# First blocks of a windowed attention: keys and queries split in three column parts, POOL's order written out, masks in one operation each, and products of zeros in TensorE's waits

## The chip, the core and the metric

The kernel runs on one core of a Trainium2 chip. The metric is the device time of one execution in microseconds (us). Besides, one execution was taken by the hardware profiler; its rows name engines as PE (TensorE matmul), PEld (TensorE weight load), DVE (VectorE), ACT (ScalarE), POOL (GpSimd) and SP (SyncE, which issues most loads).

## The reference

Attention over 4 batches of 8 heads, 768 positions of 64 numbers, where a query sees the 128 newest positions and 4 sink positions at the start; behind it a mixture of experts, in which a token may keep its predecessor's expert.

```python
def _attn_ref(q, k, v, n_sink, window):
    scores = scale * np.matmul(q, k.transpose(0, 1, 3, 2))
    is_sink = pos[None, :] < int(n_sink)
    rel = pos[:, None] - pos[None, :]
    in_window = (rel >= 0) & (rel < int(window))
    scores = np.where(is_sink | in_window, scores, -1000000000.0)
    a = np.exp(scores - np.max(scores, axis=-1, keepdims=True))
    a = a / (np.sum(a, axis=-1, keepdims=True) + 1e-09)
    return np.matmul(a, v)

def _moe_ref(x, w_gate, w_local, w1, w2):   # for each token
    e = fresh_e if s == 0 or local_gate[b, s] < 0.5 else prev_e
    h = np.maximum(x[b, s] @ w1[e], 0.0)
    out[b, s] = p[e] * (h @ w2[e])
```

## The kernel before

The attention runs in 8 groups (batch, half of the heads), each of 6 blocks of 128 queries, 48 blocks in all; the experts follow. A group has two pairs of heads, and a block two units, one for each pair. For a unit, `score` makes three products for each head: high part of the queries with high and low part of the keys, and low part of the queries with the high part of the keys. High parts are casts of the raw numbers (L132), low parts are raw minus high (L137). `out` adds the mask and takes the extreme (DVE, L616) and makes exponentials with their sums (ACT, L619). One block later `turn` transposes them (L634) and ACT copies them out of PSUM (L641); two blocks later `apply` multiplies with the values (L665, L670), three blocks later `back` and `finish` turn and scale the result (L560, L576). The order of PE, DVE and ACT in the loop over blocks is the program's; POOL's was left to the compiler's scheduler.

Raw keys and queries of a pair lie in one of four buffers and are loaded in one transfer; for group 0 in two, columns 0 to 255 (`lead`) and the rest. Which engine casts and subtracts for group 0 is in `SENG`: keys cast by DVE, subtracted by POOL, queries cast by ACT, subtracted by DVE. From group 1 on POOL does all four steps of a pair (`ENGS`); group 1's are called at blocks 3 to 5 (`HEADS`), and block 6 is the first that reads them. The keys of the sink positions meet their values in a product of their own, for which POOL prepares the value rows (`sinks`, L548 and L549) after a load of 96 KB. `setup` and `xb_meta` are small copies on POOL for the routing. Before the first block PE runs 12 products of zeros (L183), and DVE makes three masks (L206 to L214), mask2 for blocks 2 to 5, mask1 for block 1, mask0 for block 0.

Of the kernel before, what the change touches and what calls it, by code (L numbers as in the profile page):

```python
# [27 lines left out]
SK = 8  # L28
# [3 lines left out]
ROW = 516  # L32
SKIP = 1 << 20
# [39 lines left out]
def kernel(ctx, tc, qkd, vn, vs, w1, w2, nw, c_misc, c_ident, c_idw, c_small,  # L73
# [60 lines left out]
    lows, behind = {}, []  # L134

    def low(e, out, raw, hi):
        lows[e] = getattr(nc, e).tensor_tensor(out=out, in0=raw, in1=hi.bitcast(F32), op=ALU.subtract)  # L137

    def qk_split(gi, eng, ahead=True, qc=slice(0, S), kc=slice(0, KPAD)):
        def part(p, x, cs, eng):  # L140
            hi, lo = qk_t[gi % 2][p][2 * x:2 * x + 2]
            r = raw[(gi * NPR + p) % NR][:, x]
            i = copy(eng[0], hi[:, cs], r[:, cs])
# [3 lines left out]
            low(eng[1], lo[:, cs], r[:, cs], hi[:, cs])  # L147

        def keys(p):
            part(p, 1, kc, eng[p][0:2])  # L150

        def queries(p):
            part(p, 0, qc, eng[p][2:4])
            if ahead:
                qk_load(gi * NPR + p + NR)

        steps = []
        for p in range(NPR):
            steps += [lambda p=p: keys(p), lambda p=p: queries(p)]
        heads = [[(qh, kh), (qh, kl), (ql, kh)] for qh, ql, kh, kl in qk_t[gi % 2]]  # L160
        return steps, heads

    lead = 2 * P
# [3 lines left out]
    qk_load(0, slice(0, lead))  # L167
    qk_load(1, slice(0, lead))
# [4 lines left out]
    nc.sync.dma_start(v_t[0][:, 2:NBLK], vn[0, 0, :, 2:NBLK])  # L173

    zrow = const.tile([P, ROW], F32, name="zrow")
    nc.gpsimd.memset(zrow, 0.0)
    nc.gpsimd.memset(zrow.bitcast(I32)[:, 513:514], SKIP)

    with tc.tile_pool(name="ps_w", bufs=1, space=PS) as ps_w:
        wt = ps_w.tile([P, 512], F32, name="wt")  # L180
        zb = zrow.bitcast(BF16)
# [22 lines left out]
    mask = at.tile([P, N2 + 3 * P], F32, name="mask")  # L204
    mask2, mask1, mask0 = mask[:, 0:N2], mask[:, N2:N2 + 2 * P], mask[:, N2 + 2 * P:]
    nc.vector.tensor_scalar(mask2, rel, win, None, op0=ALU.is_lt)  # L206
    nc.vector.scalar_tensor_tensor(out=mask2, in0=rel, scalar=0.0, in1=mask2, op0=ALU.is_ge, op1=ALU.mult)
    nc.vector.tensor_scalar(mask2[:, P:P + SK], key, nsk, None, op0=ALU.is_lt)
    nc.vector.tensor_copy(mask1[:, 0:P], mask2[:, 0:P])
    nc.vector.tensor_copy(mask1[:, P:2 * P], mask2[:, P + SK:N2])  # L210
    nc.vector.tensor_copy(mask0, mask2[:, P + SK:N2])
    for m in (mask1, mask0):
        nc.vector.tensor_tensor(out=m[:, 0:SK], in0=m[:, 0:SK], in1=mask2[:, P:P + SK], op=ALU.max)
    nc.vector.tensor_scalar(mask, mask, BIG, -BIG, op0=ALU.mult, op1=ALU.add)  # L214

    lead0, heads0 = qk_split(0, SENG, False, slice(0, lead), slice(0, lead))
    rest0 = qk_split(0, SENG, False, slice(lead, S), slice(lead, KPAD))[0]
    with tc.issue_after(flag_op.ins) if FLAGF else ExitStack():
        for f in lead0[0:2]:
            f()  # L220

    narrow = nc.values_load(flag_i[0:1, 0:1], min_val=0, max_val=1,
                            skip_runtime_bounds_check_because="a product of comparisons")
# [234 lines left out]
    def xb_meta(b):  # L458
        xb = xb_t[b % 2]
        nc.gpsimd.tensor_copy(xb.bitcast(I32)[:, :, DM + 1], ids[:, b * NBLK:(b + 1) * NBLK])  # L460
        nc.gpsimd.memset(xb[:, :, DM + 2:ROW], 0.0)
# [50 lines left out]
    def attention(fast):  # L512
        sfx = "f" if fast else "g"
        with ExitStack() as st:
# [225 lines left out]

            if fast:
                ng = len(groups)
                preps = [{"heads": []} for _ in groups]
                preps[0]["heads"] = heads0
                gst = [group_steps(b, g, preps[gi]) for gi, (b, g) in enumerate(groups)]

                def head(gi, h):
                    if h == 0:
                        preps[gi]["steps"], preps[gi]["heads"] = qk_split(gi, ENGS)
                    preps[gi]["steps"][h]()  # L750

                def slot(u, gi, k):
                    nx = gi + 1
                    if gi == 0:
                        for x in LOADS.get(k, ()):
                            qk_load(x) if x > 1 else gst[nx]["load"][x]()
                        if k == RK:
                            gst[0]["sinks"]()
# [12 lines left out]
                    if gi:  # L771
                        last.clear()
# [27 lines left out]
                for b in range(B - 1):  # L800
# [6 lines left out]
                for f in lead0[2:]:  # L807
                    f()
                order = ExitStack()
                order.enter_context(tc.manual_schedule(engines={ET.PE, ET.DVE, ET.Activation}))  # L810

                for n in range(nb):
                    now, a, z, y = (blocks[x] if 0 <= x < nb else [] for x in (n, n - 1, n - 2, n - 3))
                    nm = f"{sfx}{n}"
                    deep = bool(a) and a[0]["i"] >= 2
                    for u in now:
                        if u["k"] == 0 and u["g"] == 0 and n:
                            xb_meta(u["b"])
                        if u["gi"] == 0 and u["k"] == 6:
                            xb_meta(0)  # L820
# [20 lines left out]
                    if a:  # L841
                        turned(a[0])
                    lo = sink_out(a[0]["blk"], tps, mm, nm) if deep else None
                    if now:
                        out(now[1])
                    for _, read, _ in todo:
# [7 lines left out]
                        lo()  # L854
                    if a:
                        invert(a[0]["blk"])
                    if n < 2:
                        for f in rest0[2 * n:2 * n + 2]:
                            f()
                    for u in now:  # L860
                        slot(u, u["gi"], u["k"])
                    if z:
# [541 lines left out]
def _layout(q, k, v, w_gate, w_local, w1, w2, n_sink, window):  # L1404
# [19 lines left out]
    p = np.arange(P)[:, None]  # L1424
    c = np.arange(P)[None, :]
    s = np.zeros((P, SK))
    rel = np.concatenate([P + p - c, s - 1, p - c], axis=1).astype(f)
# [34 lines left out]
```

## Time and profile before

| | us |
|---|---|
| median of 3 runs | 561.14 |
| lowest, highest | 560.61, 565.27 |
| the profiled execution's own time | 567.39 |
| its span, first to last instruction | 565.6 |

The profiled execution is one run, and not the fastest; durations of single instructions are read from it. Its mean granted TensorE clock is 0.963 of full speed (2.4 GHz); 0.50 means 1.2 GHz. In a timeline row the first number is the start in us from the span's start, the second the length; neighbours of one kind are merged to one row with their count, and brackets give the idle time of the engine before the row and what ended it.

### The profile page before, as it was taken

The page shows a single profiled execution, that of the slowest core. Times are in us where ns is not written, and L with a number is a line of the kernel's source. Part 1 is how long each engine was busy: PE and PEld are TensorE (multiplying, and loading weights), DVE is VectorE, ACT ScalarE, POOL GpSimd, SP SyncE. Part 2 cuts the span into 40 slices and gives each one's busy share as a digit, 9 for nine tenths or more (in the row PEclk, how much of TensorE's full clock was granted, in tenths as well). Part 3 has the DMA queues.
Part 4 walks back from the last instruction along what each step waited for, and adds up shares of the span by engine and source line. Part 5 has one row for each costly group of instructions (what it writes and reads, how often), then busy time and mean ns, then how long its engine had stood idle before and what let it go on. Part 6 is the DMA issues. An engine that isn't in the chain of part 4 may idle for free. (4 is left out here: it accounts for less than half of the span.)

```text
span 565.6 us, 11738 instructions
## 1 busy us (share of the span) xinstructions
PE 526.0 (93%) x3888; PEld 445.7 (79%) x3888; DVE 326.6 (58%) x1275; ACT 275.9 (49%) x837; POOL 227.0 (40%) x193
## 2 busy tenths in 40 slices
PE   6899999899989989999999999898999999999994
PEld 3698878787767778679988888878877698889893
DVE  4677888687868765443447282743463945353321
ACT  3688877587767961332533362605332544124120
POOL 3973543756380460343440263434402544104001
PEclk7699999899999979996999999999999999999998
DMA  8624404251443170584741474846414756110000
GB/s 303 242 116 181 154 29 180 113 181 51 164 155 128 60 235 8 194 251 143 261 132 30 140 252 139 281 116 232 150 42 130 259 186 239 56 50 32 20 24 36
DMA packets 30475, 80.47 MB, mean 142 GB/s; under 512 B 3646, under 2 KB 5310, under 8 KB 30272
## 3 DMA queue, kind: packets, MB, share of 16 engines
q1 hardware_dynamic: 25520, 65.41, 34.1%
q0 software_dynamic: 4176, 12.64, 5.9%
q14 instruction: 149, 1.22, 0.7%
q8 instruction: 54, 0.88, 0.7%
q10 hardware_dynamic: 576, 0.32, 0.2%
HBM read 63.34 MB, written 16.06 MB: 140 GB/s over the span
## 5 line engine op out<-in xcount | busy, mean ns | idle before, releaser
L619 ACT ACTIVATE pef<-smf,biasf 128x264 f32<-128x264 f32 (+2 forms) x192 | 93.6, 490 | 52.2 <-DVE biasf L616 48.7
L1150 ACT ACTIVATE hq<-h 128x32 fp32r<-128x32 f32 (+4 forms) x112 | 31.9, 315 | 148.2 <-PE h L1139 91.0
L1115 DVE SCALAR_TENSOR_TENSOR hq<-h,hq 128x32 fp32r<-128x32 f32 (+4 forms) x112 | 34.6, 333 | 71.6 <-ACT hq L1150 66.7
L616 DVE CUSTOM_DVE_ANT_0 smf<-sf,mask 128x264 f32<-128x264 f32 (+2 forms) x192 | 67.0, 402 | 11.6 <-PE sf L604 3.4
L1188 PE MATMUL late<-w_a,hq 128*128 128x512 f32 (+2 forms) x288 | 69.3, 394 | 2.2 <-issue 2.2
L1188 PEld LDWEIGHTS late<-w_a,hq 128*128 128x128 f32 (+2 forms) x288 | 50.6, 179 | 16.2 <-issue 3.4
L634 PE MATMUL tpf<-ident,pef 128*128 128x128 f32 x352 | 55.6, 292 | 3.4 <-ACT ptf L641 2.7
L1170 POOL DMA_INDIRECT out_dram<-ot_d,oi_d x18 | 18.9, 1051 | 97.3 <-DVE ot_d L1169 78.0
L670 PE MATMUL avf<-ptf,v 128*64 128x128 f32 x704 | 51.7, 288 | 0.5 <-issue 0.5
L641 ACT COPY ptf<-tpf 128x512 f32<-128x512 f32 (+1 forms) x96 | 51.0, 531 | 0.8 <-PE avf L670 0.3
L634 PEld LDWEIGHTS tpf<-ident,pef 128*128 128x128 f32 x352 | 39.2, 146 | 14.7 <-ACT ptf L641 7.2
L670 PEld LDWEIGHTS avf<-ptf,v 128*64 128x64 f32 x704 | 39.2, 141 | 5.8 <-issue 1.2
L560 PE MATMUL bkf<-idw,xtf 128*128 128x146 f32 x192 | 34.6, 304 | 6.0 <-DVE xtf L556 5.6
L1188 PE MATMUL late<-w_b,hq 128*128 128x512 f32 (+1 forms) x168 | 39.8, 393 | 0.0
L1045 POOL TENSOR_TENSOR w_c<-raw,w_c 128x1024 fp32r<-128x1024 f32 x10 | 24.9, 2498 | 34.1 <-ACT w_c L1044 23.4
L1188 PEld LDWEIGHTS late<-w_b,hq 128*128 128x128 f32 (+1 forms) x168 | 30.9, 186 | 7.1
L619 ACT ACTIVATION_READ_ACCUMULATOR pef<-smf,biasf 128x1 f32 x192 | 36.4, 190 | 0.0
L1139 PEld LDWEIGHTS h<-x_a,w_c 128*128 128x128 f32 x288 | 34.8, 192 | 1.9 <-issue 1.8
L1139 PE MATMUL h<-x_a,w_c 128*128 128x256 f32 x288 | 35.2, 283 | 1.0 <-PE late L1188 1.0
L1045 POOL TENSOR_TENSOR w_a<-raw,w_a 128x1024 fp32r<-128x1024 f32 x10 | 24.7, 2470 | 26.8 <-ACT w_a L1044 21.9
L560 PEld LDWEIGHTS bkf<-idw,xtf 128*128 128x128 f32 x192 | 27.2, 195 | 9.3 <-DVE xtf L556 9.0
L604 PE MATMUL sf<-w_a 64*128 64x264 f32 (+2 forms) x288 | 28.0, 324 | 6.2 <-DVE w_a L132 2.1
(241 smaller groups left out, 1051.9 us busy)
## 6 DMA issues: line engine op xcount, KB each, us to landing
raw<-in_dram SPq DMA_DIRECT2D x53, 512.0 KB, 4.5
raw<-in_dram SPq DMA_DIRECT2D x14, 800.0 KB, 6.2
xr_0n<-xs SPq DMA_DIRECT2D x21, 258.0 KB, 4.4
v<-in_dram SPq DMA_DIRECT2D x7, 768.0 KB
raw_w<-in_dram SPq DMA_DIRECT2D x7, 512.0 KB, 5.0
raw<-in_dram SPq DMA_DIRECT2D x10, 256.0 KB, 4.5
xs<-zrow SPq DMA_DIRECT2D x9, 258.0 KB, 5.2
xr_0r<-xs SPq DMA_DIRECT2D x8, 258.0 KB
```

Source lines behind the costliest of these rows:

```text
L560: mm = nc.tensor.matmul(bk[:, pr * WX:(pr + 1) * WX], blk["xt"][:, pr, :], idw[:, g * NPR + pr, :], start=True, stop=True, skip_group_chec ...
L604: u["mm"] = nc.tensor.matmul(sps[:, t, :w], qx[ROWS[t], i * P:(i + 1) * P], kx[ROWS[t], off:off + w], start=m == 0, stop=m == 2)
L616: u["dve"] = nc.vector.tensor_tensor_reduce(out=sm[:, :w], in0=sps[:, t, :w], in1=mk, scale=-0.125, scalar=BIG, op0=ALU.add, op1=ALU.min, ...
L619: nc.scalar.activation(pe[:, h, :w], sm[:, :w], AF.Exp, bias=bias[:, t:t + 1], scale=-1.0, accum_out=z[:, h, 0:1])
L634: nc.tensor.transpose(tp[:, t, k, :], pe[:, 2 * c + t, o:o + P], ident)
L641: nc.scalar.copy(pt[:, :, 0:nt, :], tp[:, :, 0:nt, :])
L670: nc.tensor.matmul(avt[ROWS[t], pr, :], prep["v"][:, j, 2 * pr + t, :], x["pt"][:, t, k, :], start=i < 2 and pr == 0 and k == 0, stop=pr = ...
L1045: todo += [lambda s=s: lo(out=l[:, s], in0=raw[:, s], in1=h.bitcast(F32)[:, s], op=ALU.subtract) for s in ([slice(0, FF)] if eng[1] == "po ...
L1115: nc.vector.scalar_tensor_tensor(out=d[:, :, 1, :], in0=h, scalar=0.0, in1=d.bitcast(F32)[:, :, 0, :], op0=ALU.max, op1=ALU.subtract)
L1139: nc.tensor.matmul(hs, w[:, k, fs], x, start=t == 0, stop=t == len(mm) - 1)
L1150: relu = nc.scalar.activation(d[:, :, 0, :], h, AF.Relu)
L1188: nc.tensor.matmul(o, a, w, start=t == 0, stop=t == len(mm) - 1, skip_group_check=half)
```

## The change

- Keys and queries of group 0 are split in three column parts (`CUTS`: 0 to 255, 256 to 527, 528 to the end), each loaded by a transfer of its own, the second ones ahead of the values. First part: ACT casts; DVE subtracts for pair 0, POOL for pair 1. Second part: POOL casts and subtracts for pair 0, DVE for pair 1. Third part: POOL does all.
- The order of DVE, ACT and POOL at the start is written out, and POOL's too through the first 6 blocks. The second part is called after block 0 and in block 1, the sink rows and pair 0's third part in block 1, pair 1's third part in block 2, `xb_meta` and `setup` at block 3, group 1's splits at blocks 3 to 5 as before.
- A mask is one operation (`hidden`: distance at least the window, times a large negative number; future positions get a large distance in the constant), mask1 and mask0 get their sink columns by one more (`sunk`). mask0 is made before block 0, mask1 inside it, mask2 in block 1.
- After the scores of blocks 0 to 2 PE runs nine products of 512 columns of zeros (`PAUSE`), into a bank of its own.

```diff
-SENG = (("vector", "gpsimd", "act", "vector"),) * NPR
+CUTS = 0, 2 * P, 2 * N2, KPAD
+SENG = ("act", "vector"), ("act", "gpsimd")
+MENG = ("gpsimd", "gpsimd"), ("vector", "vector")
+LENG = (("gpsimd", "gpsimd"),) * 2
+PAUSE = {(0, 0): 4, (0, 1): 1, (1, 1): 2, (2, 0): 2}
...
+    for cs in cuts[0:2]:
+        for x in range(NPR):
+            qk_load(x, cs)
     nc.sync.dma_start(v_t[0][:, 0:2], vn[0, 0, :, 0:2])
     nc.sync.dma_start(idw.rearrange("p r c -> p (r c)"), c_idw)
-    qk_load(0, slice(lead, KPAD))
-    qk_load(1, slice(lead, KPAD))
+    for x in range(NPR):
+        qk_load(x, cuts[2])
...
+    def hidden(m, d, top):
+        nc.vector.tensor_scalar(m, d, top, -BIG, op0=ALU.is_ge, op1=ALU.mult)
+
+    def sunk(m):
         nc.vector.tensor_tensor(out=m[:, 0:SK], in0=m[:, 0:SK], in1=mask2[:, P:P + SK], op=ALU.max)
...
+    for k in (0, 1):
+        for x in (1, 0):
+            parts0[0, 0, x][k]()
+    hidden(mask2[:, P:P + SK], key, nsk)
+    hidden(mask0, rel[:, P + SK:N2], win)
+    sunk(mask0)
+    for x in (1, 0):
+        for f in parts0[0, 1, x]:
             f()
...
+                def pause(n, c):
+                    if (n, c) in PAUSE:
+                        idle = ps_b.tile([P, 512], F32, tag="b", name=f"idle{n}_{c}")
+                        for _ in range(PAUSE[n, c]):
+                            nc.tensor.matmul(idle, zb[:, 0:P], zb[:, 0:512], start=True, stop=True)
+
+                between = {0: [lambda: hidden(mask1.rearrange("p (a c) -> p a c", a=2), sides(misc), win),
+                               lambda: sunk(mask1)]}
+                after = {0: [*parts0[1, 0, 1], *parts0[1, 0, 0], *parts0[1, 1, 1]],
+                         1: [*parts0[1, 1, 0], lambda: hidden(sides(mask), sides(misc), win), gst[0]["sinks"],
+                             *parts0[2, 0, 1], *parts0[2, 0, 0]],
+                         2: [*parts0[2, 1, 1], *parts0[2, 1, 0]]}
                 order = ExitStack()
-                order.enter_context(tc.manual_schedule(engines={ET.PE, ET.DVE, ET.Activation}))
+                order.enter_context(tc.manual_schedule(engines={ET.PE, ET.DVE, ET.Activation, ET.Pool}))
...
+                    if n == NBLK:
+                        order.close()
+                        order.enter_context(tc.manual_schedule(engines={ET.PE, ET.DVE, ET.Activation}))
...
                         score(u)
+                        pause(n, u["c"])
```

In `parts0[c, p, x]` the three indices are column part, pair, and 1 for keys or 0 for queries; each entry is a cast and a subtraction.

## Rows read from the trace of the kernel before

**Rows 1.** The page's first lines: busy time of PE, DVE, ACT and POOL with their share of the span; the granted clock in 40 equal slices, in tenths.

```profile
PE 526.0 (93%) x3888; PEld 445.7 (79%) x3888; DVE 326.6 (58%) x1275; ACT 275.9 (49%) x837; POOL 227.0 (40%) x193
PEclk7699999899999979996999999999999999999998
```

**Rows 2.** Busy time of each engine in short stretches of the start: stretch, length, busy time and instructions of each engine, granted clock, DMA share, GB/s.

```profile
10.00:15.00 5.00, 3.35 (x20) 2.58 (x21) 2.49 (x11) 2.03 (x9) 3.23 (x6) 0.50 1.03 407
15.00:20.00 5.00, 3.31 (x14) 2.09 (x15) 3.72 (x13) 3.23 (x14) 5.00 (x5) 0.50 1.02 397
20.00:25.00 5.00, 5.00 (x32) 4.10 (x31) 2.84 (x15) 3.48 (x12) 5.00 (x6) 0.50 0.08 28
25.00:26.00 1.00, 1.00 (x10) 1.00 (x9) 0.17 (x3) 0.83 (x3) 1.00 (x1) 0.85 0.59 109
```

**Rows 3.** The timeline of TensorE up to block 2: products of zeros (L183) with two rows of their weight loads, then scores (L604).

```profile
1.33 4.46 PE L183 MATMUL wt<-zrow 128*128 128x512 bf16 x12 [1.33 <-POOL sum_z L186]
...
4.30 0.15 PEld L183 LDWEIGHTS <-zrow 128*128 128x128 bf16 x1 [0.28 <-issue]
4.72 0.58 PEld L183 LDWEIGHTS <-zrow 128*128 128x128 bf16 x3 [0.28 <-issue]
5.89 0.83 PE L604 MATMUL sf<-w_a 64*128 64x128 f32 x6
10.89 2.31 PE L604 MATMUL sf<-w_a 64*128 64x128 f32 x16 [1.57 <-POOL w_a L137]
...
15.02 1.23 PE L604 MATMUL sf<-w_a 64*128 64x264 f32 x6 [0.78 <-DVE biasf L616]
```

**Rows 4.** The timeline of TensorE at blocks 4 to 6: scores (L604) and the transposes (L634) of the block before.

```profile
27.34 1.00 PE L604 MATMUL sf<-w_a 64*128 64x264 f32 x12
28.27 1.09 PE L634 MATMUL tpf<-ident,pef 128*128 128x128 f32 x8
...
31.10 0.98 PE L604 MATMUL sf<-w_a 64*128 64x264 f32 x12
...
34.85 0.89 PE L604 MATMUL sf<-hq 64*128 64x128 f32 x12
35.67 1.09 PE L634 MATMUL tpf<-ident,pef 128*128 128x128 f32 x8
```

**Rows 5.** The timeline of ACT and DVE at the start: casts of keys and queries, the last mask operation, exponentials, a copy of transposes.

```profile
4.76 0.41 ACT L132 CAST w_a<-raw 128x256 fp32r<-128x256 f32 x1 [1.26 <-DMA raw<-in_dram]
5.96 0.41 ACT L132 CAST w_a<-raw 128x256 fp32r<-128x256 f32 x1 [0.80 <-DMA raw<-in_dram]
7.58 0.50 DVE L214 TENSOR_SCALAR mask<-mask 128x648 f32<-128x648 f32 x1
8.40 0.29 DVE L132 CAST w_a<-raw 128x256 fp32r<-128x256 f32 x1 [0.32 <-DVE mask L214]
14.57 0.51 ACT L619 ACTIVATE pef<-smf,biasf 128x256 f32<-128x256 f32 x1 [1.22 <-DVE biasf L616]
15.07 0.50 ACT L619 ACTIVATE pef<-smf,biasf 128x256 f32<-128x256 f32 x1
20.73 0.59 ACT L641 COPY ptf<-tpf 128x512 f32<-128x512 f32 x1 [0.18 <-PE tpf L634]
```

**Rows 6.** The timeline of POOL at the start: a small copy, pair 1's key subtraction, the sink rows, a subtraction of group 1's keys.

```profile
9.39 0.19 POOL L460 COPY xb<-small 128x6 int32<-128x6 int32 x1 [3.33 <-DMA small<-in_dram]
9.93 0.19 POOL L460 COPY xb<-small 128x6 int32<-128x6 int32 x1
10.11 0.72 POOL L137 TENSOR_TENSOR w_a<-raw,w_a 128x256 fp32r<-128x256 f32 x1
12.44 0.39 POOL L548 CAST srf<-sxf 96x256 fp32r<-96x256 f32 x1 [1.61 <-DMA sxf<-in_dram]
12.91 0.73 POOL L549 TENSOR_TENSOR srf<-sxf,srf 32x256 fp32r<-32x256 f32 x1
18.42 2.33 POOL L137 TENSOR_TENSOR hq<-raw,hq 128x800 fp32r<-128x800 f32 x1
```

**Rows 7.** POOL's casts (L132) and subtractions (L137) up to 60 us, one row for each shape: count, busy us in all, mean ns of one, idle time before them.

```profile
L137 POOL TENSOR_TENSOR w_a<-raw,w_a 128x800 fp32r<-128x800 f32 x2 | 3.8, 1906 | 0.0
L137 POOL TENSOR_TENSOR w_a<-raw,w_a 128x768 fp32r<-128x768 f32 x2 | 3.7, 1827 | 0.0
L132 POOL CAST w_a<-raw 128x800 fp32r<-128x800 f32 x2 | 1.7, 852 | 0.7 <-DVE biasf L616 0.7
L132 POOL CAST w_a<-raw 128x768 fp32r<-128x768 f32 x2 | 1.7, 826 | 3.0 <-PE sf L604 3.0
L137 POOL TENSOR_TENSOR w_a<-raw,w_a 128x256 fp32r<-128x256 f32 x2 | 1.5, 740 | 3.5 <-DVE w_a L132 3.5
```

**Rows 8.** Busy time of each engine in later stretches around waits of TensorE, columns as in rows 2 (the last but two is the granted clock).

```profile
104.00:107.00 3.00, 1.49 (x12) 0.98 (x10) 1.08 (x4) 0.87 (x3) 2.32 (x3) 1.00 0.57 224
107.00:108.00 1.00, 1.00 (x6) 1.00 (x6) 0.05 (x1) 0.00 (x0) 0.76 (x1) 0.61 0.52 198
...
200.00:206.00 6.00, 5.83 (x38) 5.14 (x39) 4.11 (x21) 4.25 (x13) 5.36 (x5) 0.50 0.48 128
155.00:158.00 3.00, 1.47 (x11) 0.98 (x10) 0.85 (x4) 0.64 (x3) 2.08 (x4) 1.00 0.46 178
158.00:159.00 1.00, 1.00 (x14) 0.93 (x15) 0.29 (x3) 0.00 (x0) 1.00 (x2) 1.00 0.69 264
```

More of the change, by code (lines that the diff above doesn't have):

```diff
@@ L132, in copy, with qk_part, high @@
         return (nc.scalar.copy if e == "act" else getattr(nc, e).tensor_copy)(out, in_)
-    lows, behind = {}, []
+    behind = []
     def low(e, out, raw, hi):
[L137 to L143, printed above, removed]
+        getattr(nc, e).tensor_tensor(out=out, in0=raw, in1=hi.bitcast(F32), op=ALU.subtract)
+    def qk_part(gi, p, x, eng, cs=slice(0, KPAD)):
+        cs = slice(cs.start, min(cs.stop, KPAD if x else S))
+        hi, lo = (t[:, cs] for t in qk_t[gi % 2][p][2 * x:2 * x + 2])
+        r = raw[(gi * NPR + p) % NR][:, x, cs]
+        def high():
+            i = copy(eng[0], hi, r)
             if behind:
@@ L146, in part, with qk_heads, qk_split, step @@
                     mybir.DependencyClass.Sync, mybir.DependencyReason.DATA), reason="a port of its own")
[L147 to L154, printed above, removed]
-                qk_load(gi * NPR + p + NR)
[L157 to L163, printed above, removed]
+        return high, lambda: low(eng[1], lo, r, hi)
+    def qk_heads(gi):
+        return [[(qh, kh), (qh, kl), (ql, kh)] for qh, ql, kh, kl in qk_t[gi % 2]]
+    def qk_split(gi, eng):
+        def step(p, x):
+            for f in qk_part(gi, p, x, eng[p][2 - 2 * x:4 - 2 * x]):
+                f()
+            if not x:
+                qk_load(gi * NPR + p + NR)
+        return [lambda p=p, x=x: step(p, x) for p in range(NPR) for x in (1, 0)]
+    cuts = [slice(a, z) for a, z in zip(CUTS, CUTS[1:])]
     v_t = [at.tile([P, NBLK, HG, D], F32, name=f"v{t}") for t in range(2)]
     idw = at.tile([P, H // 2, WX], F32, name="idw")
-    qk_load(0, slice(0, lead))
-    qk_load(1, slice(0, lead))
+    for cs in cuts[0:2]:
+        for x in range(NPR):
+            qk_load(x, cs)
     nc.sync.dma_start(v_t[0][:, 0:2], vn[0, 0, :, 0:2])
     nc.sync.dma_start(idw.rearrange("p r c -> p (r c)"), c_idw)
-    qk_load(0, slice(lead, KPAD))
-    qk_load(1, slice(lead, KPAD))
+    for x in range(NPR):
+        qk_load(x, cuts[2])
     nc.sync.dma_start(v_t[0][:, 2:NBLK], vn[0, 0, :, 2:NBLK])
+    begin = ExitStack()
+    begin.enter_context(tc.manual_schedule(engines={ET.DVE, ET.Activation, ET.Pool}))
     zrow = const.tile([P, ROW], F32, name="zrow")
@@ L202, with sides @@
                                              op0=ALU.is_le, op1=ALU.mult)
[L204 to L212, printed above, removed]
-        nc.vector.tensor_tensor(out=m[:, 0:SK], in0=m[:, 0:SK], in1=mask2[:, P:P + SK], op=ALU.max)
[L214 to L219, printed above, removed]
+    mask = at.tile([P, N2 + SK + 3 * P], F32, name="mask")
+    mask2, mask1, mask0 = mask[:, 0:N2], mask[:, N2 + SK:N2 + SK + 2 * P], mask[:, N2 + SK + 2 * P:]
+    def sides(t):
+        return t[:, 0:N2 + SK].rearrange("p (a c) -> p a c", a=2)[:, :, 0:P]
+    def hidden(m, d, top):
+        nc.vector.tensor_scalar(m, d, top, -BIG, op0=ALU.is_ge, op1=ALU.mult)
+    def sunk(m):
+        nc.vector.tensor_tensor(out=m[:, 0:SK], in0=m[:, 0:SK], in1=mask2[:, P:P + SK], op=ALU.max)
+    parts0 = {(c, p, x): qk_part(0, p, x, eng[p], cuts[c])
+             for c, eng in enumerate((SENG, MENG, LENG)) for p in range(NPR) for x in (1, 0)}
+    for k in (0, 1):
[6 more added lines that the diff above has]
+        for f in parts0[0, 1, x]:
             f()
+    begin.close()
     narrow = nc.values_load(flag_i[0:1, 0:1], min_val=0, max_val=1,
@@ L460, in xb_meta @@
         nc.gpsimd.tensor_copy(xb.bitcast(I32)[:, :, DM + 1], ids[:, b * NBLK:(b + 1) * NBLK])
[L461 removed]
+        return nc.gpsimd.memset(xb[:, :, DM + 2:ROW], 0.0)
     w_buf = [w_a]
@@ L742, in attention @@
                 ng = len(groups)
-                preps = [{"heads": []} for _ in groups]
-                preps[0]["heads"] = heads0
+                preps = [{"heads": qk_heads(gi)} for gi in range(ng)]
                 gst = [group_steps(b, g, preps[gi]) for gi, (b, g) in enumerate(groups)]
@@ L748, in head @@
                     if h == 0:
-                        preps[gi]["steps"], preps[gi]["heads"] = qk_split(gi, ENGS)
+                        preps[gi]["steps"] = qk_split(gi, ENGS)
                     preps[gi]["steps"][h]()
@@ L815, in attention @@
                     deep = bool(a) and a[0]["i"] >= 2
+                    if n == NBLK:
+                        order.close()
+                        order.enter_context(tc.manual_schedule(engines={ET.PE, ET.DVE, ET.Activation}))
                     for u in now:
                         if u["k"] == 0 and u["g"] == 0 and n:
-                            xb_meta(u["b"])
+                            with tc.issue_after(metas[-1].ins):
+                                metas.append(xb_meta(u["b"]))
                         if u["gi"] == 0 and u["k"] == 6:
-                            xb_meta(0)
+                            metas.append(xb_meta(0))
                             setup()
@@ L843, in attention @@
                     lo = sink_out(a[0]["blk"], tps, mm, nm) if deep else None
+                    for f in between.get(n, []):
+                        f()
                     if now:
@@ L856, in attention @@
                         invert(a[0]["blk"])
-                    if n < 2:
-                        for f in rest0[2 * n:2 * n + 2]:
-                            f()
+                    for f in after.get(n, []):
+                        f()
                     for u in now:
@@ L1426, in _layout @@
     s = np.zeros((P, SK))
-    rel = np.concatenate([P + p - c, s - 1, p - c], axis=1).astype(f)
+    rel = np.concatenate([P + p - c, s - 1, p - c], axis=1)
+    rel = np.where(rel < 0, SKIP, rel).astype(f)
     key = (s + np.arange(SK)).astype(f)
```

8 lines of the change are left out of this document (2 added, 6 removed).

## The prediction, before the result was known

> **What bounds the kernel now.** I read the page's engine sums first: TensorE is busy 93% of the span, and its granted clock is low only in a few slices, the first ones above all [rows 1]. So a change to the first blocks pays only through the moment at which TensorE's unbroken work begins, and through the clock. The table of short stretches shows that moment: from 10 to 20 us TensorE is busy 3.35 and 3.31 of 5 us at half clock (1.2 GHz), from 20 us on it is busy all the time, and only in the 25th microsecond does the clock come back to 2.4 GHz [rows 2]. The order in time on TensorE says what it waits for: the score of block 0 comes in pieces, the first at 5.89 and the last at 10.89 us, released by POOL; block 2 begins at 15.02 [rows 3]. From block 4 on blocks follow each other every 3.76 us (27.34, 31.10, 34.85) with no gap, and the transposes that follow block 6's score start at 35.67 [rows 4]. That 35.67 is my mark: the score of block 6 is the first to read group 1's keys and queries, and all later work hangs on this flow. What the change gains is how much earlier the mark comes.
>
> **Part by part: the first 256 columns.** Before, pair 1's last query part is held up twice. VectorE casts its keys at 8.40, behind the masks that end at 8.08 [rows 5]; POOL subtracts at 10.11 for 0.72, behind small copies that waited until 9.39 for a load [rows 6]. After, ACT casts all four: pair 0 from 4.76, pair 1 from 5.96, 0.41 each [rows 5]. VectorE subtracts for pair 0; POOL has only pair 1's two, 0.74 each [rows 7], from 6.4 to 7.9. Three short mask operations stand ahead of block 0 instead of nine up to 8.08. Block 0's score is complete at 8.3 instead of some 11.3 (10.89 and the products left): 3 us won here. The small setup copies stand now at block 3; their 0.54 us (9.39 to 9.93, estimated from four starts) is counted below.
>
> **Blocks 0 to 3.** Block 1 needs no more columns; blocks 2 and 3 need the second part (272 columns), of which POOL makes pair 0 and VectorE pair 1. From 8.3 on ACT sets the pace: exponentials are 0.50 apart (14.57, 15.07) [rows 5], so a unit of two costs 1.0. Block 0's last two end at 9.5; the four units of blocks 1 and 2 and three copies of transposes (up to 0.59 each [rows 5], taken as 0.5) lie between, with 0.5 for the wide mask: 9.5 + 4.0 + 1.5 + 0.5 = 15.5, when block 2's transposes can start. Those of block 3 started at 28.27 before [rows 4]; now 15.5 + 3.76 = 19.3, nine earlier. Going on at 3.76, the mark would come at 26.8, a gain of 8.9.
>
> **The zero products.** Nine products of 512 columns lie in waits of TensorE; in the warm-up one starts 0.43 after another (512 columns: 1.2 GHz), and after 4.72 us three weight loads of 0.15 fit in 0.58, 0.21 apart (2.4 GHz) [rows 3]. So they take 1.9 together. They hide in the wait for pair 1 and in ACT's pace; were that cover gone, they would cost 1.9. The warm-up used the same zeros, so zeros do raise the clock. Should the clock fall at 8 us as before, TensorE would come to block 6 up to 3 us later, which the next paragraph hides.
>
> **POOL in a fixed order: the new bound.** Before, POOL took group 1's splits whenever it was free, the first ones ahead of group 0's rest. Now everything stands in line through block 5, and group 1's four splits come last. The line: second part of pair 0, two casts and two subtractions. A cast of 272 columns I take as 0.40 (between 0.39 for 256 on 96 partitions [rows 6] and 0.85 for 800 [rows 7]), a subtraction as 0.75 (between 0.74 for 256 and 1.91 for 800 [rows 7]), and 0.08 lies between a cast and its own subtraction (12.44 + 0.39, then 12.91 [rows 6]): 2.4, until 10.3. Then the sink rows, whose load lands only at 12.44 [rows 6]; the bytes queued ahead of it are the same as before, so POOL stands still for 2.1 us with all else behind it. Sink rows 0.39 + 0.08 + 0.73 + 0.08: 13.7. Third part, two pairs of 272 and 240 columns, 2.3 each: 18.3. Setup copies 0.5: 18.8. Group 1, for each pair keys 0.85 + 0.08 + 1.91 and queries 0.83 + 0.08 + 1.83 [rows 7], 5.5 less small overlaps; two pairs 10.9: **29.7**. Block 6's second score ends with the product of the last of these parts, so the mark comes at about 29.9, not 26.8, and the gain is 35.67 - 29.9 = **5.8**. Bounds: with the sink load already there POOL ends at 27.6; with every POOL row stretched like the 800-column subtraction beside a VectorE subtraction (2.33 against 1.91 [rows 6, 7]), 22%, at 33.2. I take the unstretched rows, since POOL's rows beside VectorE's ordinary block work are the 1.83 and 1.91 ones.
>
> [...]
>
> **What the stall costs in clock.** TensorE reaches block 6 at about 25.5 and has little to do until 29.9. Stretches of such thinness were followed by a fall: half busy from 104 to 107 us, half clock from 107.2 on; the same busy time from 155 to 158 us was not followed by one [rows 8]. Once low, the clock stayed so while TensorE was busy 5.83 of 6 us [rows 8]. Here the thin stretch is longer, so I expect the fall, with some 4.2 us of full work done at half rate: 2.1 lost (bounds 0 and 3.0, the latter half of the 6 us at the low level from 200 to 206 [rows 8]). [...]
>
> **How the numbers follow.** Against the profiled execution (567.39): 567.39 - 5.8 + 2.1 = 563.7. That execution is 6.3 above the median of 561.14; its later half-clock stretches lie outside the change. One thing differs inside: the clock came back at 25 us though TensorE was fully busy from 20 us [rows 2], and other runs may get it back sooner; I take 0.6 off for it. Forecast: 561.14 - 5.8 + 2.1 + 0.6 = **558.0**.
>
> **The rivals.**
> - POOL bounds block 6, but the clock holds: 555.9. For it: 155 to 158 us [rows 8]. Against: the thin stretch is longer here, 4 us with one short burst in it. Chance 0.2.
> - POOL does not bound it, because the sink load lands before 10.3 and the overlaps are larger than I took: the mark at 26.8, 561.14 - 8.9 + 0.6 = 552.8. Against: 12.44. Chance 0.12.
> - Slower: POOL's line is stretched by VectorE. At the 22% above the line ends at 33.2; with the 27% by which 2.33 exceeds 1.83 on the 16.0 us that follow the sink rows, at 34.0, and with the 0.2 and the 2.1 behind it at 36.3, 0.6 past 35.67: 561.14 + 0.6 + 0.6 = 562.3. The sign turns where the line ends later than 33. Against: nothing on VectorE after 12.5 is of that kind. Chance 0.08.
> - The zero products do not keep the clock, so the change does not do what it says there: TensorE arrives later, there is less stall, and the mark stays at 29.9 or comes up to 2 later: 556 to 560. Chance 0.05.
> - The forecast has 0.55.
>
> The range 552.5 to 562.5 takes in all but the tails of these. A change of under 1% (5.6 us) is about what a measurement of this kernel can tell from none. Faster by more than that: the second rival, a third of the first, and the forecast's lower tail, 0.25; slower by more: 0.03; within: 0.72.
>
> **What would show it.** In the changed profile: block 0's score complete near 8.3; block 2's transposes near 15.5; POOL idle some 2 us before the sink cast at 12.4; POOL's last 768-column subtraction ending near 29.7 with TensorE idle before it; transposes after block 6's score near 29.9; half clock shortly after. The prediction is wrong if POOL is done before TensorE gets there, if the sink load lands much earlier, or if blocks 0 to 3 take longer than 15.5.

## The result: 1% slower, and the profile after

The changed kernel takes 570.25 us (median of 20 executions, 565.15 to 576.61); the kernel before, run beside it, 566.66 (20 executions). The ratio is 1.0106 (95% interval 1.0076 to 1.0136), so the change costs some 6 us. The forecast was 558.0, with a range up to 562.5. A ratio leaves out executions over 1.5% above the fastest of their kernel; medians take in all. The profiled execution of the changed kernel took 571.05, with a span of 569.3. Line numbers have moved: score L618, `out` L630 and L633, transposes L648, casts L135, subtractions L140, sinks L562 and L563, zero products L822.

The page's sums and the granted clock after, which answer to [rows 1]:

```profile
PE 527.5 (93%) x3897; PEld 445.3 (78%) x3897; DVE 326.9 (57%) x1270; ACT 275.4 (48%) x837; POOL 230.0 (40%) x203
...
PEclk9969999999989999995999999999999999999998
```

TensorE's work is the same. The low clock of the first slices is gone (7 6 before), a lower one (6) stands in the third slice, from 28 us on, and one (5) in the 19th, at 256 us and later.

TensorE's timeline after, first blocks, then block 6 (start, length, operation, count, idle time before and what ended it), which answers to [rows 3, 4]:

```profile
6.00 0.55 PE L618 MATMUL sf<-w_a 64*128 64x128 f32 x6
...
7.45 0.65 PE L618 MATMUL sf<-w_a 64*128 64x128 f32 x6
...
15.74 0.66 PE L648 MATMUL tpf<-ident,pef 128*128 128x128 f32 x4
...
26.97 0.55 PE L618 MATMUL sf<-hq 64*128 64x128 f32 x6
29.14 0.62 PE L618 MATMUL sf<-hq 64*128 64x128 f32 x4 [1.62 <-POOL hq L135]
35.27 0.47 PE L618 MATMUL sf<-hq 64*128 64x128 f32 x2 [5.51 <-POOL hq L140]
35.67 1.97 PE L648 MATMUL tpf<-ident,pef 128*128 128x128 f32 x8
...
40.28 0.98 PE L618 MATMUL sf<-hq 64*128 64x256 f32 x12
```

Block 0 is scored at 8.10, and block 6 begins at 26.97, 7.9 us earlier than before (34.85). Then TensorE stands idle for 1.62 and 5.51 us, both ended by POOL, and the mark comes at 35.67: to the hundredth where it was. The whole lead is spent in these waits.

POOL's timeline after, which answers to [rows 6]:

```profile
9.35 0.85 POOL L140 TENSOR_TENSOR w_a<-raw,w_a 128x272 fp32r<-128x272 f32 x1
12.93 0.41 POOL L562 CAST srf<-sxf 96x256 fp32r<-96x256 f32 x1 [2.73 <-DMA sxf<-in_dram]
...
18.18 0.70 POOL L140 TENSOR_TENSOR w_a<-raw,w_a 128x240 fp32r<-128x240 f32 x1
...
19.36 0.86 POOL L135 CAST hq<-raw 128x800 fp32r<-128x800 f32 x1
...
25.64 0.83 POOL L135 CAST w_a<-raw 128x768 fp32r<-128x768 f32 x1
26.43 1.89 POOL L140 TENSOR_TENSOR hq<-raw,hq 128x800 fp32r<-128x800 f32 x1
28.26 0.82 POOL L135 CAST hq<-raw 128x768 fp32r<-128x768 f32 x1
29.27 0.85 POOL L135 CAST w_a<-raw 128x800 fp32r<-128x800 f32 x1 [0.19 <-DVE biasf L630]
30.09 1.80 POOL L140 TENSOR_TENSOR w_a<-raw,w_a 128x768 fp32r<-128x768 f32 x1
31.83 1.62 POOL L135 CAST w_a<-raw 128x800 fp32r<-128x800 f32 x2
33.41 1.80 POOL L140 TENSOR_TENSOR hq<-raw,hq 128x768 fp32r<-128x768 f32 x1
```

Here one reads tile names. Group 0 and group 2 share the tiles `w_a`, group 1 has `hq`. The last four pieces of group 1 should stand together; instead pieces of group 2 (`w_a`, 768 or 800 columns wide) stand between them: casts of 0.83, 0.85 and 1.62 us and a subtraction of 1.80, 5.10 together. They are called in block 6 and later, and their order against group 1's was the compiler's. TensorE needs the subtraction that ends at 35.21.

Busy time by stretch after, columns as in [rows 2] (granted clock before the DMA share):

```profile
20.00:25.00 5.00, 5.00 (x53) 4.20 (x52) 4.12 (x19) 3.81 (x14) 4.92 (x7) 1.00 0.16 66
25.00:30.00 5.00, 3.14 (x36) 2.57 (x33) 3.32 (x19) 4.09 (x15) 4.81 (x5) 0.92 0.80 297
30.00:36.00 6.00, 0.73 (x4) 0.62 (x5) 0.21 (x1) 0.00 (x0) 6.00 (x7) 0.50 0.08 30
36.00:40.00 4.00, 4.00 (x29) 3.87 (x29) 1.18 (x8) 1.72 (x7) 4.00 (x3) 0.56 0.87 283
```

TensorE works 0.73 of 6 us at the stall, its granted clock falls to 0.50, and the full work behind it runs at 0.56. From the mark to block 7 it takes 4.61 us (35.67 to 40.28); before, 2.83 (35.67 to 38.50). So block 7 is 1.8 us late. TensorE's timeline of before at block 7:

```profile
38.50 0.97 PE L604 MATMUL sf<-hq 64*128 64x256 f32 x12
```

### The profile page after: what moved, and what is told of

It reads as the page before. It is cut to its first block, busy times and chain, and to the rows that moved or that the text cites. A ratio compares the mean times of both kernels' runs of the same rounds, so it can differ in the third digit from the quotient of the medians.

```text
span 569.3 us, 11764 instructions
## 1 busy us (share of the span) xinstructions
PE 527.5 (93%) x3897; PEld 445.3 (78%) x3897; DVE 326.9 (57%) x1270; ACT 275.4 (48%) x837; POOL 230.0 (40%) x203
## 3 DMA queue, kind: packets, MB, share of 16 engines
q14 instruction: 148, 1.21, 0.7%
## 5 line engine op out<-in xcount | busy, mean ns | idle before, releaser
L633 ACT ACTIVATE pef<-smf,biasf 128x264 f32<-128x264 f32 (+2 forms) x192 | 93.6, 490 | 49.0 <-DVE biasf L630 49.0
L630 DVE CUSTOM_DVE_ANT_0 smf<-sf,mask 128x264 f32<-128x264 f32 (+2 forms) x192 | 67.0, 402 | 17.8 <-PE sf L618 7.5
L648 PE MATMUL tpf<-ident,pef 128*128 128x128 f32 x352 | 55.7, 289 | 5.8 <-ACT ptf L655 5.1
L648 PEld LDWEIGHTS tpf<-ident,pef 128*128 128x128 f32 x352 | 38.2, 144 | 18.3 <-ACT ptf L655 11.3
L633 ACT ACTIVATION_READ_ACCUMULATOR pef<-smf,biasf 128x1 f32 x192 | 36.3, 189 | 0.0
L590 DVE TENSOR_TENSOR xb<-bkf,rsf 128x256 f32<-128x256 f32 x48 | 20.3, 422 | 24.8 <-ACT ptsf L665 22.0
```

The costliest lines, as they stand in the source:

```text
L590: nc.vector.tensor_tensor(out=xb[:, i, g * HG * D:(g + 1) * HG * D].rearrange("p (r t d) -> p r t d", r=NPR, t=2), in0=av[:, :, 0:P].rearr ...
L630: u["dve"] = nc.vector.tensor_tensor_reduce(out=sm[:, :w], in0=sps[:, t, :w], in1=mk, scale=-0.125, scalar=BIG, op0=ALU.add, op1=ALU.min, ...
L633: nc.scalar.activation(pe[:, h, :w], sm[:, :w], AF.Exp, bias=bias[:, t:t + 1], scale=-1.0, accum_out=z[:, h, 0:1])
L648: nc.tensor.transpose(tp[:, t, k, :], pe[:, 2 * c + t, o:o + P], ident)
```

## The experiments

Each was timed in one job with 35 executions of the kernel before (medians 564.42 for the first four, 564.58 for the next four, 563.28 for the last four). "Mark" and "block 7" (start of its score) are of the profiled execution, in us.

| kernel | median | ratio to before (95%) | mark | block 7 |
|---|---|---|---|---|
| before | 564.4, 564.6, 563.3 | 1 | 35.67 | 38.50 |
| changed | 570.25 | 1.0106 (1.0076 to 1.0136) | 35.67 | 40.28 |
| e1 order written through block 7 | 561.75 | 0.9962 (0.9914 to 1.0011) | 30.81 | 36.12 |
| e2 no zero products | 563.41 | 1.0033 (0.9992 to 1.0073) | 35.74 | 41.05 |
| e3 POOL left to the compiler | 563.12 | 1.0007 (0.9972 to 1.0042) | 31.99 | 34.82 |
| e4 group 1 in two column parts | 559.67 | 0.9877 (0.9830 to 0.9925) | 27.82 | 30.94 |
| e5 changed, again | 569.22 | 1.0095 (1.0053 to 1.0138) | 35.88 | 40.69 |
| e6 clock held through the stall | 561.83 | 0.9990 (0.9953 to 1.0027) | 36.54 | 39.37 |
| e7 e4 without zero products | 562.16 | 0.9922 (0.9876 to 0.9968) | 27.28 | 30.20 |
| e8 e1 with the sinks later | 560.21 | 0.9939 (0.9897 to 0.9980) | 28.85 | 31.96 |
| e9 changed, zeros at the first expert | 565.43 | 1.0045 (1.0014 to 1.0075) | 35.95 | 41.17 |
| e10 e4, zeros at the first expert | 557.95 | 0.9911 (0.9879 to 0.9943) | 27.21 | 30.33 |
| e11 e4 with group 0 in two parts | 561.79 | 0.9987 (0.9947 to 1.0027) | 30.13 | 33.25 |
| e12 before, zeros at the first expert | 564.44 | 1.0027 (0.9989 to 1.0064) | 35.50 | 38.33 |

### Is it the order, or where the order ends? (e1, e3)

e1 lets POOL's written order run two blocks longer:

```diff
-                    if n == NBLK:
+                    if n == NBLK + 2:
```

> The changed kernel with POOL's written order kept two blocks longer, through block 7, so that group 2's casts and subtractions can't stand among group 1's. Mark: start of the transposes after block 6's score. Theory A (group 2's pieces, some 5.1 us of them, stand ahead of group 1's last subtraction): that subtraction ends at 35.2 - 5.3 = 29.9, the mark comes at 30.1 instead of 35.7, and block 7's score at 40.3 - 5.6 = 34.7 or a little more, if the clock falls as well; the time goes down by 4 to 6 us against the changed kernel, to some 0.5% below the kernel before. Theory B (the fixed order itself, by its waits between a cast and its own subtraction, makes POOL late): the mark stays at 34 or later.

POOL's timeline of e1 at the end of group 1, then TensorE's at the mark:

```profile
27.64 0.82 POOL L135 CAST hq<-raw 128x768 fp32r<-128x768 f32 x1
28.54 1.81 POOL L140 TENSOR_TENSOR hq<-raw,hq 128x768 fp32r<-128x768 f32 x1
30.29 0.40 POOL L562 CAST srf<-sxf 96x256 fp32r<-96x256 f32 x1
```

```profile
30.40 0.47 PE L618 MATMUL sf<-hq 64*128 64x128 f32 x2 [1.45 <-POOL hq L140]
30.81 1.97 PE L648 MATMUL tpf<-ident,pef 128*128 128x128 f32 x8
...
36.12 1.02 PE L618 MATMUL sf<-hq 64*128 64x256 f32 x12
```

Nothing of group 2 stands among group 1's pieces any more, the last one ends at 30.35, and the mark comes 4.9 us earlier. The fixed order itself was not at fault; its end was. By the pace the clock fell here too: the eight transposes at the mark take 1.97 us, as in the changed kernel (0.56 from 36 to 40 us there), against 1.09 before; from mark to block 7 it is 5.31 us, 2.5 above 2.83. By ratio e1 lies 1.4%, 8 us, below the changed kernel, more than the 4 to 6 expected; block 7 accounts for 4.2 of them.

e3 takes POOL out of both written orders:

```diff
-    begin.enter_context(tc.manual_schedule(engines={ET.DVE, ET.Activation, ET.Pool}))
+    begin.enter_context(tc.manual_schedule(engines={ET.DVE, ET.Activation}))
...
-                order.enter_context(tc.manual_schedule(engines={ET.PE, ET.DVE, ET.Activation, ET.Pool}))
+                order.enter_context(tc.manual_schedule(engines={ET.PE, ET.DVE, ET.Activation}))
```

> The changed kernel with POOL's order left to the compiler everywhere, as in the kernel before; parts, masks and zeros stay. Here all of group 1's subtractions stand ahead of group 2's pieces, but the casts of the later parts stand ahead of the second part's subtractions. Theory A: group 1's last subtraction ends at about 28.5; blocks 2 to 5 come some 3 us later than in the changed kernel, and the mark lies at 30 to 31, so block 7's score comes 4 to 5 us earlier than in the changed kernel. Theory B (fixed order as such is bad, not what is mixed in): about the same, so this run tells A from B only together with the one that keeps the order longer.

The mark came 1 us later than expected, at 31.99, but 3.7 before that of the changed kernel. POOL is done with group 1 at 28.92. In exchange the casts of group 0's third part and the small copies stand ahead of the second part's subtractions: block 2 waits 2.41 us for one of these, and block 3 starts at 19.96 (14.81 in the changed kernel). TensorE reaches block 6 only at 31.17, behind POOL, so there is no stall (2.83 from mark to block 7). Its time is that of the kernel before all the same; the section on the late half clock comes back to that.

### What POOL's line can give (e4, e8, e11)

e4 writes POOL's order out through block 13 and splits group 1 in two column parts, the narrow parts of both pairs first, since block 6 reads only those (two changes at once; e1 shows the first of them by itself, as far as block 7):

```diff
+CUT1 = slice(0, 2 * P), slice(2 * P, KPAD)
...
+                first1 = {6: two(0, 0) + two(0, 1), 9: two(1, 0), 10: two(1, 1)}
...
-                    if n == NBLK:
+                    if n == NBLK + 8:
```

> POOL's order kept through block 13, and group 1's keys and queries split in two column parts: the first 256 columns of both pairs first (eight operations, 1.2 us for a cast and its subtraction, 4.8 us in all), the rest behind. Theory A: POOL is done with what block 6 reads at 19.4 + 4.8 = 24.2, before TensorE gets there at 27; the mark comes at 27.8 instead of 35.7, no idle stretch of TensorE, no fall of the clock there, block 7's score at 30.6 (10 us earlier than in the changed kernel), and the time 8 us below the kernel before (1.4%). If the rest of the parts comes late for block 8 (POOL ends at 24.2 + 8.1 = 32.3, block 8 begins at 33.8) up to 1 us of it is lost. Theory B: POOL is late again and the mark is past 30.

TensorE's timeline of e4 at block 6:

```profile
27.00 0.88 PE L619 MATMUL sf<-hq 64*128 64x128 f32 x12
27.82 1.38 PE L649 MATMUL tpf<-ident,pef 128*128 128x128 f32 x8
...
30.94 0.98 PE L619 MATMUL sf<-hq 64*128 64x256 f32 x12
```

No wait is left at block 6: the twelve products follow each other, the mark lies at 27.82, 7.9 us before that of both kernels, and the work behind it keeps the pace of full clock: at 29.91 sixteen products with the values take 1.09 us, as in e6, where the granted clock is 1.00. It is the fastest by ratio, 1.2% below the kernel before.

e8 is e1 with the sink rows called behind the third part:

```diff
-                         1: [*parts0[1, 1, 0], lambda: hidden(sides(mask), sides(misc), win), gst[0]["sinks"],
+                         1: [*parts0[1, 1, 0], lambda: hidden(sides(mask), sides(misc), win),
...
-                         2: [*parts0[2, 1, 1], *parts0[2, 1, 0]]}
+                         2: [*parts0[2, 1, 1], *parts0[2, 1, 0], gst[0]["sinks"]]}
```

> The kernel with POOL's order written through block 7, and the sinks' cast and subtraction moved behind the third column part, so that POOL no longer waits some 2.7 us for their load at 10 us. Theory (POOL's line without a gap sets the mark): all later splits move up by 2.2 to 2.7 us, mark 28.1 to 28.6 against 30.8, block 7 at 31 to 34 by whether the clock falls. Rival (group 1's loads or TensorE itself come last once POOL is early): mark 29.5 or later, with the stall's end put down to a load or to PE.

POOL is done with group 1 at 27.92 instead of 30.35: the 2.73 us of waiting were real. The mark, 28.85, is a little later than expected, because TensorE is now the last and comes to block 6 at 28.03 instead of 26.88. Why shows in VectorE's timeline, a cast and a mask operation of e1, where POOL waits for the sink rows at that time, then the same two of e8:

```profile
11.98 0.27 DVE L135 CAST w_a<-raw 128x272 fp32r<-128x272 f32 x1
...
12.64 0.35 DVE L218 TENSOR_SCALAR mask<-misc,scal 128x256 f32<-128x256 f32 x1
```

```profile
12.02 0.80 DVE L135 CAST w_a<-raw 128x272 fp32r<-128x272 f32 x1
...
13.30 0.85 DVE L218 TENSOR_SCALAR mask<-misc,scal 128x256 f32<-128x256 f32 x1
```

In e8 they run beside POOL's third part, which formerly came later, and block 2's second score waits 0.64 us for the cast. With the subtraction between them (0.53 instead of 0.44) VectorE takes 1.1 us more, which is what TensorE is later at block 6.

e11 is e4 with group 0 in two column parts instead of three:

```diff
-CUTS = 0, 2 * P, 2 * N2, KPAD
+CUTS = 0, 2 * P, KPAD
...
-             for c, eng in enumerate((SENG, MENG, LENG)) for p in range(NPR) for x in (1, 0)}
+             for c, eng in enumerate((SENG, MENG)) for p in range(NPR) for x in (1, 0)}
```

> The two-part kernel with group 0's columns in two parts (0 to 255, and the rest) in place of three; the second part is made where the middle part was, by POOL for pair 0 and VectorE for pair 1. Working: POOL's two casts and two subtractions of the rest cost 0.57 + 1.27 + 0.53 + 1.19 + gaps, 3.7 us from 8.0, so pair 0 is there at 11.7 instead of 10.3, and VectorE is held for 3.1 us in place of 1.8 ahead of block 1's extremes. If the middle part matters: blocks 2 to 6 are 1 to 2.5 us later and the mark at 28.8 to 30.3; time 1 to 2.5 us above the two-part kernel. If it does not: mark 27.8.

The mark moved from 27.82 to 30.13, block 7 by 2.3 us: the middle part is worth that much, as worked out, once POOL's line behind it does not eat it. The ratio went up by 1.1%, 6 us, where 1 to 2.5 were expected; what makes up the rest stays open.

### Do the zero products matter? (e2, e7, e6)

e2 is the changed kernel, e7 is e4, both with `PAUSE = {}`.

> The changed kernel without the nine products of zeros behind the scores of blocks 0 to 2. Theory A (POOL sets the mark): the mark stays at 35.7 within 0.3 us whatever the clock does before, and the time is that of the changed kernel within 0.3%. Theory C (the zeros matter): the clock falls at about 8 us, blocks 1 to 4 come 2 to 4 us later than with the zeros, and the mark moves past 36.

> The two-part kernel (POOL's written order to block 13, group 1 in two column parts) without its nine zero products. Theory that they do nothing: mark 27.8, block 7 at 30.9, and the same time within 0.4%. Rival (with the gaps of blocks 1 to 3 empty TensorE falls to half clock there): a low stretch between 8 and 16 us, mark up to 1 us later, time 1 to 4 us more.

Stretches of e2, then of e7:

```profile
10.00:15.00 5.00, 3.85 (x36) 2.76 (x36) 4.72 (x24) 3.93 (x17) 1.90 (x5) 1.00 1.02 379
```

```profile
10.00:15.00 5.00, 3.93 (x24) 3.19 (x26) 4.07 (x23) 4.56 (x17) 1.93 (x4) 0.66 0.99 377
```

In e2 the clock held without them (1.00), in e7 it fell for a while (0.66 over these 5 us), and neither had lost anything by it at block 6: from block 0 to block 7 e7 takes 24.4 us (5.80 to 30.20), e4 24.4 (6.56 to 30.94); blocks 1 to 6 of e2 start within 0.2 us of the changed kernel's. In blocks 1 to 3 TensorE's waits end on VectorE and ACT: in e2 0.71 us twice for VectorE's extremes, 0.44 for its cast, 0.45 for a copy of ACT. e7's ratio lies 0.45% above e4's, with intervals that overlap. e2's time missed what was expected: its ratio is 1.0033, 0.7% or 4 us below that of the changed kernel, though its block 7 is 0.8 us later. So the difference arises later, and no run ties it to the zeros.

e6 puts 30 zero products between block 6's two scores, into the stall:

```diff
-PAUSE = {(0, 0): 4, (0, 1): 1, (1, 1): 2, (2, 0): 2}
+PAUSE = {(0, 0): 4, (0, 1): 1, (1, 1): 2, (2, 0): 2, (6, 0): 30}
```

> The changed kernel with 30 more zero products between the two scores of block 6, where TensorE stands idle for 5.5 us until POOL has subtracted group 1's last query split. Theory: the mark is POOL's and stays at 35.7, TensorE keeps full clock through the stall, and block 7 starts at 35.7 + 2.8 = 38.5, 1.8 us before the changed kernel and as before the change; ratio to the changed kernel 0.997. Rival (the clock falls for another reason, or the zero products delay the score behind them): block 7 at 40.3 or later.

TensorE's timeline of e6:

```profile
27.91 6.65 PE L822 MATMUL idle<-zrow 128*128 128x512 bf16 x29 [0.38 <-DVE ptsf L669]
34.49 0.44 PE L618 MATMUL sf<-hq 64*128 64x128 f32 x4
36.28 0.33 PE L618 MATMUL sf<-hq 64*128 64x128 f32 x2 [1.36 <-POOL hq L140]
36.54 1.09 PE L648 MATMUL tpf<-ident,pef 128*128 128x128 f32 x8
```

The mark is 0.9 later than expected (POOL waited 0.84 us for a load of group 2 here), but the clock holds (1.00 from 28 to 40 us) and block 7 follows after 2.83 us, as undisturbed. So the 1.8 to 2.5 us behind the stall are the clock's and nothing else's. (The trace has records of 29 of the 30 products.) By ratio e6 lies 1.0%, 6 us, below the changed kernel measured beside it, where 0.3% was expected; block 7 accounts for 1.3 of them.

### The other 4 us: half clock at the first expert (e5, e9, e12, e10)

By the traces the changed kernel owes 1.8 us at block 7, the timing says 6. e5 is the changed kernel again, in another job.

> The changed kernel itself, without an edit, to place it beside the experiments in one job. By the traces it owes 1.8 us at block 7's start and the rest is half-clock stretches that come and go: so 1.000 to 1.007 of the kernel before. If it comes again at 1.010 or more, something besides the mark and the clock costs it 3 us or more, which its trace has not shown. Mark (the transposes behind block 6's score) 35.7, block 7 at 40.3.

It came at 1.0095, so the 6 us are no accident of one job, and block 7 at 40.69 explains 2.2 of its 5.4. The rest has to lie later. Each execution lists its span and mean granted clock; span x (1 - clock) is what half clock took from TensorE. Over the executions that the ratio counts its median is 14.5 us for the kernel before (second job) and 15.9 for the changed one, both times. But in the profile of before, half of 17.1 us of it, 8.5, lies in the first 26 us [rows 2], and after, half of 10.2, 5.1, lies around the stall; both are already counted in the start of block 7. What is left, an estimate, is 6.0 before and 10.8 after: 4.8 us more lost to half clock late in the kernel (over all executions the medians are 16.9 and 16.2 or 15.9, and the difference is 2.4 to 2.7). With the 1.8 at block 7 that makes 4.2 to 6.6, against 6.0 (4.3 to 7.7) timed. For e2 the same remainder is 8.4, for e6 7.3, which goes with their smaller times; for e3 it is 10.1, and so its earlier block 7 does not show in its time. The estimate is rough: in the same way e2 would lie 2 to 6 us above the kernel before, and it lies 1.9 above it.

The traces show one place. TensorE's timeline of the changed kernel where it enters the branch of the first expert, then a stretch behind it, columns as in [rows 2]:

```profile
249.72 3.91 PE L1276 MATMUL late<-w_b,hq 128*128 128x512 f32 x16
256.35 9.03 PE L1156 MATMUL h<-x_b,w_a 128*128 128x128 f32 x48 [2.72 <-issue]
```

```profile
260.00:264.00 4.00, 4.00 (x21) 4.00 (x20) 1.85 (x8) 0.78 (x3) 3.94 (x2) 0.50 0.40 153
```

TensorE waits 2.72 us for nothing that the trace names, and the 48 products behind it take 9.03 us instead of the 5.52 to 5.60 that they take in e1 and e2. This wait differs from one kernel's profile to another: 0, 0.75 and 1.14 us in e2, e11 and e1, with no fall behind it (1.00 from 236 to 280 us in e2); 1.3 to 2.7 us in the changed one, e3, e4, e5, e7 and e8, each with 14 to 20 us of half clock behind it. In the kernel before and in e6 TensorE enters the branch without a wait and stands idle later, in the middle of the 48 products, for 1.40 and 1.21 us, until VectorE is done with a piece of `hq`; 10 and 14 us of half clock follow. TensorE's timeline of before:

```profile
249.25 2.79 PE L1128 MATMUL h<-x_b,w_a 128*128 128x128 f32 x24
253.44 4.86 PE L1128 MATMUL h<-x_b,w_a 128*128 128x128 f32 x24 [1.40 <-DVE hq L1115]
```

There it was VectorE that came late: its first piece starts 3.17 us behind TensorE's first product (252.42 and 249.25), in e2 1.11 behind (253.14 and 252.03). In e6 it was ACT, whose first piece starts 2.27 us behind the sum that it reads (254.87 and 252.60), in e2 0.39 (253.53 and 253.14). The expectations below take these two waits and those of TensorE at the entry for the same one.

e9, e12 and e10 put eight zero products ahead of the branch:

```diff
+    entry = ps_h.tile([P, 512], F32, tag="h", name="entry")
+    for _ in range(ENTRY):
+        nc.tensor.matmul(entry, zrow.bitcast(BF16)[:, 0:P], zrow.bitcast(BF16)[:, 0:512], start=True, stop=True)
     for e in range(E):
```

> The changed kernel with eight products of zeros on TensorE behind the last late product, ahead of the branch into the first expert. In the ten profiles so far TensorE stands idle there for 0 to 2.7 us, ended by nothing that the trace names, and after a gap of 1.2 us or more its clock was low for 10 to 20 us. Theory (this stretch is what sets the changed kernel's loss above the 2 us at block 7): the zeros (1.7 us at full clock) lie in the gap, the clock holds, and the time falls by 4 to 7 us against the changed kernel, to 0.996 to 1.003 of the kernel before. [...]

> The kernel before with the same eight products of zeros ahead of the first expert. If they hold the clock there, it falls to 557 to 561 (0.985 to 0.995), and the changed kernel with these zeros lies 1.5 to 3 us above it, by the later start of block 7 alone. If the changed kernel with the zeros still lies 5 us above it, its loss is not in that stretch.

> The same eight products of zeros in the two-part kernel (POOL's written order to block 13, group 1 in two column parts). Theory: mark 27.8, no half clock at the first expert, some 5 us below the two-part kernel: about 554, 0.978 to 0.985 of the kernel before. [...]

The same place in e9:

```profile
252.47 1.67 PE L1355 MATMUL entry<-zrow 128*128 128x512 bf16 x7
254.16 5.60 PE L1157 MATMUL h<-x_b,w_a 128*128 128x128 f32 x48
```

The zeros fill the wait (seven of the eight have a record), the products follow at once and at full clock, in all three profiles (5.60 us for the 48; 1.00 from 248 to 264 us in e9). The loss to half clock, by medians as above, falls from 15.9 to 10.1 in the changed kernel, from 15.1 to 12.9 in the kernel before, from 8.3 to 6.4 in e4. In time that was less than expected: the changed kernel came down from 1.0095 to 1.0045, less than the 4 to 7 us; the kernel before, expected at 557 to 561, did not gain at all (1.0027): in its profile TensorE had no wait at the entry to put the zeros in, so their 1.7 us may well have cost about what the half clock gave back. Besides, in e12's profile TensorE stands idle for 4.51 us at a later step (264.52, no releaser named), and 3.4 us of half clock go with it. e10, expected 5 us below e4, is not faster by ratio (0.9911 against 0.9877; 557.95 against 559.67 by median, so no difference can be told). But with the zeros in both, the changed kernel lies 1.0 us above the kernel before (565.43 and 564.44; ratios 0.2% apart, each within some 0.35%), and no longer 5 to 6. That points to this stretch for most of what exceeds the 2 us at block 7; the drop itself, some 4 us, is known only to 3 or 4. Why the stretch should cost the changed kernel more than the kernel before, e2 or e6, whose code is the same there, stays open: in the single profiles half clock took 5.1 us there before, and 6.8 in the changed kernel and in e6.

## Why the prediction was wrong, point by point

- **What bounds it, and the mark: right.** Block 6's score was where the lead was kept or lost, in the changed kernel as in e1, e4, e8 and e11.
- **The first blocks: right.** Block 0 scored at 8.10 (8.3 predicted), block 2's transposes at 15.74 (15.5), POOL idle 2.73 us (2.1) ahead of the sink cast at 12.93 (12.44), third part done at 18.88 (18.3), the second part at 10.20 (10.3). Only the pace behind them was not 3.76: blocks 3 to 6 start 4.25, 3.98 and 3.93 apart (14.81, 19.06, 23.04, 26.97), so TensorE reached block 6 at 26.97 instead of 25.5, which POOL hid.
- **POOL's line: the step that failed is "group 1's four splits come last".** I took the order of the diff for the order on the engine. It holds for the pieces inside it among themselves; behind its end, at block 6, stands work that the compiler could move forward, and it placed 5.1 us of group 2's pieces among the last of group 1's. The term of 5.8 us became 0. In the trace of before, group 2's first casts came at 31.87, behind all of group 1's, after 2.99 us of waiting for block 5's score; but it also had the sink cast of group 1 (22.26) ahead of three of group 1's subtractions, and the prediction did not ask what else POOL could be given. Where the assumption is made true, in e1, the same sum holds: POOL's end at 30.35 (29.7), the mark at 30.81 (29.9), 0.9 off, of which 0.6 was already there at 18.88.
- **The stall and the clock: right in kind and size.** 2.1 predicted; 1.8 in the changed kernel, 2.5 in e1 and e2, nothing where the stall was filled (e6) or absent (e3).
- **The zero products: no effect on the mark either way**, as the prediction had priced them; the fear that TensorE would come late without them was empty, too. Their effect on the whole time is not shown: e2 lies 0.7% below the changed kernel, e7 0.45% above e4. The 1.2 and 2.4 GHz that the prediction read in the warm-up are 512 columns in 0.43 and in 0.21 us, the spacing of the weight loads alone: the profile has the clock as a share of full speed, and its records of before start at 4.81 us, with 1.00 up to 8.23 and 0.50 behind it.
- **The rival on the slower side had the sign and the place, not the mechanism.** POOL's line did end at 35.21, but none of group 1's pieces was stretched: the 768-column subtractions took 1.80 to 1.83. Beside VectorE's second part POOL lost next to nothing, a 272-column subtraction of 0.85 (0.77 at 17.01), and its second part ended at 10.20; VectorE lost, the same subtraction taking 0.89 at 9.61 beside POOL's and 0.44 at 12.38 with POOL idle. VectorE's timeline of the changed kernel:

```profile
9.61 0.89 DVE L140 TENSOR_TENSOR w_a<-raw,w_a 128x272 fp32r<-128x272 f32 x1
...
12.38 0.44 DVE L140 TENSOR_TENSOR w_a<-raw,w_a 128x272 fp32r<-128x272 f32 x1
```

POOL's subtraction began first (9.35, VectorE's at 9.61), and in e8 VectorE's cast of 0.80 (12.02) began behind POOL's subtraction of 11.96.
- **Transposes and the clock.** The clock was 1.00 from 20 to 25 us, through blocks with eight transposes each, and in e2 from 5 to 25 us without the zeros. The eight transposes take 1.3 of a block's 3.9 us there, and no run here shows the clock under transposes alone.
- **The base.** 561.14 was a median of 3; the same kernel has medians of 563.3 to 566.7 in four jobs. 5.5 of the 12.3 us between forecast and result lie there. For the change itself the sum said -3.1, the ratio says +6.0: of these 9.1 the missing gain is 5.8 and the late half clock, which no term covered, an estimated 2.4 to 4.8; the clock's 2.1 came out 0.3 smaller. That makes 7.9 to 10.3. The 0.6 for the start is shown by no run.

## What to carry to other kernels

When part of an engine's order is written out by hand, ask what stands behind the end of that part, and count it as competing work: a lead of 8 us was lost because an order ended too early, and two blocks more of it gave back 4.9. Read tile names, not line numbers, when pieces of several groups share a line of code. And split what the next stage waits for, so that it gets the piece it reads first (e4), before tuning what fills the waits.

## What was not expected of the hardware

TensorE's wait at the branch into the first expert differed from profile to profile, 0 to 2.7 us, and those of 1.3 us and more were followed by 14 to 20 us of half clock, which took 3.4 us from the first 48 products alone (9.03 against 5.6). In two profiles VectorE or ACT came late there in its place, and TensorE waited a step later. The same kernel's executions lie 10 us apart (557.88 to 568.04 for the 35 of before in the first job); how much of that is this wait was not separated. The trace names no releaser, so what ends the wait is not shown; in e9, with 1.67 us of zeros queued ahead of the branch, TensorE goes from them to the 48 products without a wait.
